# A feed-forward kernel whose mirrored half is finished on VectorE: reading one PSUM bank out in the middle of its sum, in place of splitting the sum over two banks

## The chip, the cores and the metric

The kernel runs on one core of one Trainium2 chip. The metric is device time in microseconds (us) of one execution. The four runs of the kernel before lie within 0.35% (629.28 to 631.47 us). A verdict needs 2%: below that the word is "same", and we then go by the interval of the ratio.

TensorE is written PE in the profile, its weight loads PEld, VectorE DVE, ScalarE ACT, GpSimd POOL and SyncE SP; "POOLq" and "SPq" are their queues as issuers of DMAs. PSUM is the memory that the matmuls of these kernels sum into; a bank here is one tile of it, 128 x 512 numbers (`xb` in the profile).

## The reference, cut to what matters

```python
def _attn_ref(x):                       # x: 8 x 3008 x 256
    X = np.fft.fft(x, axis=1)
    X = np.fft.fft(X, axis=2)
    return X.real.astype(np.float32)

def _moe_ref(x, w_in, w_out):           # 24064 x 256, 256 x 2048, 2048 x 256
    h = np.maximum(x @ w_in, 0.0)
    return (h * h @ w_out).astype(np.float32)
```

The real part of a two-dimensional Fourier transform has mirrored rows. The row at frequency k and the row at S−k share the same two partial sums, one even (a cosine part, called `pt`) and one odd (a sine part, `qt`). The hidden layer is then `even + odd` for the one row and `even − odd` for the mirror. The kernel computes the two partial sums once and makes both rows from them.

## The kernel before: the parts that matter

The work after the transform goes in 25 chunks of columns (numbered from 0; the full ones are 512 pairs wide, the first two 256 and the last 264). Each full chunk has 16 steps, and in each step one unit of 128 hidden features is started, the unit of two steps ago is finished, and eight small matmuls (`po`) of the second layer for the chunk before are mixed in. There are two ways to make a unit.

```python
def x_front(c, u):                       # the normal unit: one bank, three passes of TensorE
    xb = psx.tile(...)                   # one PSUM bank of six
    ... mm(xb, G1, PT) ; mm(xb, G2, QT)  # even + odd
    act(r_s(c, u), xb, AF.Relu)          # ScalarE: first half of h
    return (c, u, xb, None)

def x_back(cur):                         # two steps later (LAG = 2)
    ... mm(xb, G3, QT)                   # G3 = -2*G2: even - odd, in the same bank
    relu_d(c, u, lambda o, i: act(o, xb[:, :, i], AF.Relu))   # ScalarE: mirrored half

def x_split(c, u):                       # the split unit: two banks, two passes
    ... mm(xo, G2, QT) ; mm(xe, G1, PT)
    act(bs[0], xo, AF.Copy)              # ScalarE: odd part to SBUF
    def add():                           # VectorE, one step later
        stt(out=bs[1], in0=ebc[c], scalar=gE2[:, u:u+1], in1=bs[0], op0=mult, op1=subtract)
        sat(r_s(c, u), xe, bs[0])        # saturating add: relu(even + odd)
        relu_d(..., sat(o, xe, bs[1]))   # saturating add: relu(even - odd)
    return (c, u, None, add)
# ... (cuts)
YZ = [(0,0)]*3 + [(2,0)]*3 + [(5,1)]*9 + [(7,1)]*9 + [(0,0)]   # split units, ScalarE squares, per chunk
```

A split unit saves TensorE one pass and costs VectorE three operations. `eb` (`ebc[c]`) is the last row of `qt` copied over all partitions, and its product with `gE` repairs one feature row that carries a different sign. VectorE also squares h (`h<-h`, 128x2048) and makes the transform of the next batches. In the timelines read here VectorE works in the order of the program, whatever has to wait: in run 1 below it stands still for 3.25 us before one saturating add, and behind that add waits a piece of the transform (`v<-u`, started at 330.14 us) whose operand had been complete since 323.64 us.

Of the kernel before, what the change touches and what calls it, by code (L numbers as in the profile page):

```python
# [10 lines left out]
F32 = mybir.dt.float32  # L11
# [13 lines left out]
def kernel(  # L25
# [103 lines left out]
    for s in range(2):  # L129
        gather(0, 1 - s)  # L130
        nc.sync.dma_start(out=x4[0:NP, s, :, :], in_=up(0, s))
    jrow = iota("jrow", [P, P], [[1, P]], 1, 0)
    idx2 = iota("idx2", [P, 1], [[0, 1]], NQ // 2 * (NP - 1), -NQ // 2, I32)
# [56 lines left out]
    def dmats():  # L190
        pv = nc.gpsimd
        t = tgp.tile([P, P], F32, name="td", tag="td")
        m = tgp.tile([P, P], F32, name="md", tag="md")
        pv.tensor_scalar(out=m, in0=jrow, scalar1=pidx[:, 0:1], scalar2=None, op0=ALU.mult)
        pv.tensor_scalar(out=t, in0=m, scalar1=1.0 / D, scalar2=R23, op0=ALU.mult, op1=ALU.add)
        pv.tensor_scalar(out=t, in0=t, scalar1=R23, scalar2=-float(D),
                         op0=ALU.subtract, op1=ALU.mult)
        pv.tensor_tensor(m, m, t, op=ALU.add)
        pv.memset(csD[:, 0, 0, P - 1 : P], 1.0)

        def fin():
            absval(t, m)
            nc.vector.tensor_copy(csD[:, 0, 1, P - 1 : P], alt)
            act(csD[:, 0, 1, 0 : P - 1], m[:, 0 : P - 1], AF.Sin, bias=0.0, scale=wD)
            act(csD[:, 0, 0, 0 : P - 1], t[:, 0 : P - 1], AF.Sin, bias=hpi[:, 0:1], scale=-wD)

        def hi():
            ts(out=csD[:, 1, :, 0:P:2], in0=csD[:, 0, :, 0:P:2], scalar1=-1.0, scalar2=None,
               op0=ALU.mult)
            nc.vector.tensor_copy(csD[:, 1, :, 1:P:2], csD[:, 0, :, 1:P:2])  # L210
        return fin, hi
# [88 lines left out]
    def gmat(c):  # L300
        cs = slice(c * 512, (c + 1) * 512)
        pc = psx.tile([P, 512], F32, name="pc", tag="x")
        for t in range(2):
            mm(pc, cosD[:, t, :], win16(c)[:, t, :], t == 0, t == 1)
        ps = psx.tile([P, 512], F32, name="ps", tag="x")
        for t in range(2):
            mm(ps, sinD[:, t, :], win16(c)[:, t, :], t == 0, t == 1)
        act(G1[:, cs], pc, AF.Copy, bias=0.0, scale=1.0 / HS)
        act(G2[:, cs], ps, AF.Copy, bias=0.0, scale=-1.0 / HS)

# [3 lines left out]

    eall = const.tile([P, 2, NQ, B], F16, name="eall")
    bf = {}
# [88 lines left out]
    def stage1_ops(b, blk, inline_e=False, run=3):  # L405
# [31 lines left out]
        return ops  # L437

    def e_ops(bs):
        nb = len(bs)  # L440
# [14 lines left out]
        for blk in range(2):  # L455
            ops += dft_ops(blk, lambda par, blk=blk: [
                (nb, lambda q: eall[k, blk, q, bs[0] : bs[0] + nb], q, cosT)
                for q in range(par, NQ, 2)], nb, (None, fin(blk)))
# [23 lines left out]

    YZ = [(0, 0)] * 3 + [(2, 0)] * 3 + [(5, 1)] * 9 + [(7, 1)] * 9 + [(0, 0)]

    def plan(c, y, z):
        if chunks[c][1] != CH:
            return (), ()
        return ([u for u in range(NFC) if (u * y + 8) % NFC < y],
                [p for p in range(NFC // 2) if (p * z + 4) % (NFC // 2) < z])

    PLAN = [plan(c, *YZ[c]) for c in range(len(chunks))]

# [7 lines left out]
    def e_double():  # L500
        ts(out=gE2, in0=gE, scalar1=2.0, scalar2=None, op0=ALU.mult)

# [9 lines left out]
    def mm2_ops(c):  # L512
# [48 lines left out]
        def one(grp, j, fc):  # L561
            s, t0, m = grp[j]

            def f():
                if j == 0 and fc == 0:
                    st["o"] = pso.tile([P, 2, D], F32, name="po", tag="po")
                o = n + n % P + t0 if s == 1 else t0
                w = 2 * m if s == 2 else m
                mm(st["o"][0:w, j, :], h2v(c, fc // nf)[:, fc % (2 * nf), o : o + w], wout16[:, fc, :],
# [25 lines left out]
    def x_front(c, u):  # L595
# [3 lines left out]
        for j in range(nf):  # L599
            fs = slice((u * nf + j) * P, (u * nf + j + 1) * P)  # L600
            for sn, G in ((0, G1), (1, G2)):
                for (b, i, o, l) in segs:
                    mm(xb[:, j, o : o + l], G[:, fs], PQ[b][sn][:, i : i + l],
                       j == 0 and sn == 0 and o == 0, sn == 1)
        act(r_s(c, u), xb, AF.Relu)  # L605
        return (c, u, xb, None)
# [3 lines left out]
    def e_spread(c):  # L610
        g0, n, nf, segs = chunks[c]
        ebc[c] = esp.tile([P, CH], F16, name="eb", tag="eb", bufs=2)
        for (b, i, o, l) in segs:
            nc.gpsimd.dma_start(out=ebc[c][:, o : o + l],  # L614
                              in_=PQ[b][1][P - 1 : P, i : i + l].unsqueeze(1).to_broadcast([1, P, l]))

    nsplit = [0]

    def x_split(c, u):
        g0, n, nf, segs = chunks[c]  # L620
        fs = slice(u * P, (u + 1) * P)
        xs = [psx.tile([P, 512], F32, name=nm, tag="x")[:, 0:n] for nm in ("xo", "xe")]
        for t, G, sn in ((xs[0], G2, 1), (xs[1], G1, 0)):
            for (b, i, o, l) in segs:
                mm(t[:, o : o + l], G[:, fs], PQ[b][sn][:, i : i + l], o == 0, True)
        nsplit[0] += 1
        bs = tgp.tile([P, 2, CH], F32, name="bs", tag=("tt", "tm")[nsplit[0] % 2])
        bs = [bs[:, j, 0:n] for j in range(2)]
        act(bs[0], xs[0], AF.Copy, bias=0.0, scale=1.0)  # L629

        def add():
            stt(out=bs[1], in0=ebc[c][:, 0:n], scalar=gE2[:, u : u + 1], in1=bs[0], op0=ALU.mult,  # L632
                op1=ALU.subtract)

            def sat(o, t):
                nc.vector._custom_dve(TENSOR_ADD_SAT, out=o, in0=xs[1], in1=t, s0=BIG, s1=0.0)  # L636

            sat(r_s(c, u)[:, 0, :], bs[0])
            relu_d(c, u, lambda o, i: sat(o[:, 0, :], bs[1]))
        return (c, u, None, add)  # L640

    def x_back(cur):
        c, u, xb = cur[:3]
        if xb is None:
            return
        g0, n, nf, segs = chunks[c]
        for j in range(nf):
            fs = slice((u * nf + j) * P, (u * nf + j + 1) * P)
            for (b, i, o, l) in segs:
                mm(xb[:, j, o : o + l], G3[:, fs], PQ[b][1][:, i : i + l], False, True)  # L650
        relu_d(c, u, lambda o, i: act(o, xb[:, :, i], AF.Relu))  # L651

    def x_square(cur):
# [3 lines left out]
        h2 = h2v(c, u)  # L657
        if u // 2 in PLAN[c][1]:
            nf = chunks[c][2]
# [74 lines left out]
    ST1 = {0: (0.66, 0.98)}  # L734
    EGRP = {1: [2, 3, 4], 4: [5, 6, 7]}
    for b in range(B - 1):
        s0 = first_step[b]
        L = first_step[b + 1] - s0
        at = lambda z: s0 + int(z * (L - 1))
        for bb, lo, hi in FOLD.get(b, []):  # L740
            spread(sum(fold_ops(bb), []), at(lo), at(hi))
        side.setdefault(at(0.0) + 1, []).append(lambda bb=b + 1: alloc_pq(bb))
# [10 lines left out]
    for si, (c, u) in enumerate(steps):  # L753
        if u == 0 and PLAN[c][0]:
            side.setdefault(si - 3, []).append(lambda c=c: e_spread(c))

# [15 lines left out]
    for si, (c, u) in enumerate(steps):  # L772
# [4 lines left out]
        take = [mmq.pop(0) for _ in range(-(-len(mmq) // max(1, due - si)))]  # L777
        flight.append((x_split if u in PLAN[c][0] else x_front)(c, u))
        h = len(take) // 2
# [10 lines left out]
        if len(made) > SQ:  # L790
            retire()
        if len(flight) > 1 and flight[-2][3]:
            flight[-2][3]()
        for f in side.get(si, []):
            f()
    if flight[-1][3]:
        flight[-1][3]()
    while flight:
# [42 lines left out]
```

## Time and profile before

| | before |
|---|---|
| time, median of the runs beside the changed kernel | 630.06 us (629.28 to 631.47) |
| TensorE busy | 606.4 us of a span of 628.5 |
| VectorE busy | 536.8 us |
| ScalarE busy | 479.3 us |
| TensorE, 396 to 588 us | 192.00 of 192 us |

First the busy times of the whole page, and the shares of the chain of work that ended last (the chain is followed back from the last instruction, at each step to what released it):

```profile
PE 606.4 (96%) x4682; PEld 446.9 (71%) x4682; DVE 536.8 (85%) x827; ACT 479.3 (76%) x872; POOL 68.8 (11%) x97
...
PE 92%; DVE 6%; ACT 1%; issue 0%; DVEq 0%; POOL 0%; POOLq 0%; ACTq 0%
```

Next the table of windows for one long late stretch. The columns are the window, its length, then the busy time of PE, PEld, DVE, ACT and POOL with counts, the granted clock, the DMA share and GB/s:

```profile
396.00:588.00 192.00, 192.00 (x1505) 146.25 (x1504) 180.16 (x243) 149.67 (x258) 4.83 (x9) 1.00 0.30 50
```

TensorE has no gap. VectorE is busy for 94% of the stretch.

The groups of VectorE instructions that matter (busy us, mean ns of one | idle before them, and what ended most of it):

```profile
L663 DVE TENSOR_TENSOR h<-h 128x2048 f16<-128x2048 f16 (+1 forms) x174 | 207.8, 1195 | 41.1 <-ACT h L651 36.5
L636 DVE CUSTOM_DVE_ANT_0 h<-xe,bs 128x512 f16<-128x512 f32 x228 | 145.9, 680 | 0.0
L632 DVE SCALAR_TENSOR_TENSOR bs<-eb,gE,bs 128x512 f32<-128x512 f16 x114 | 85.0, 745 | 9.1 <-ACT bs L629 8.4
```

The means are the lengths of single records. What an instruction costs its engine is the distance to the next start when the next one waits for nothing. In this trace that is 1135 ns for the square, 600 for the saturating add and 663 for the add L632: each about 82 ns less than its record.

Last, the timeline around one group of narrow matmuls. The weights `eall` are 127 rows by 3 columns here:

```profile
142.95 0.60 PE L73 MATMUL po<-wout,h 128*128 128x256 f16 x4
143.48 0.64 PE L73 MATMUL pf<-cosT,eall 127*3 127x377 f16 x3
144.06 0.39 PE L73 MATMUL xb<-pt,G 128*128 128x512 f16 x1
```

Four `po` matmuls stand 109 ns apart, so the next should start at 143.39; it starts at 143.48. The same happens on the way back to full-width weights. I count 18 such changes, 1.75 us in all.

### The profile page before, as it was taken

To read this page: it belongs to the slowest core of one execution; us is meant where nothing else is said; L and a number is where in the kernel's file an instruction comes from. 1 tells how busy PE (TensorE), PEld (TensorE's weight loads), DVE (VectorE), ACT (ScalarE), POOL (GpSimd) and SP (SyncE) were. 2 spreads that over 40 slices of the span, in tenths; PEclk is the share of its full clock that TensorE was granted. 3 is DMA by queue.
4 is the path that set the end of the run, shared out by engine and by line. 5 is a ranking of instruction groups with operands and counts; after the bars stand their busy time and mean duration, and the time that the engine had idled before them with its cause. 6 is when DMAs were issued, how large, how long until landed. Compare 5 with 4: busy or idle time off the path is not lost.

```text
span 628.5 us, 11983 instructions
## 1 busy us (share of the span) xinstructions
PE 606.4 (96%) x4682; PEld 446.9 (71%) x4682; DVE 536.8 (85%) x827; ACT 479.3 (76%) x872; POOL 68.8 (11%) x97
## 2 busy tenths in 40 slices
PE   3969999999999999999999999999999999999997
PEld 1547677776777777777777768777787778877786
DVE  8788799995988989889899879998999899999920
ACT  6768887777788788777887877877877778878871
POOL 8204043120120005000000000000000000000000
PEclk9979999999999999999999999999999999999999
DMA  8944477682591416714313314314233134131112
GB/s 282 300 83 138 120 181 205 156 225 57 91 208 36 59 44 170 138 34 59 43 51 44 57 34 63 43 47 48 54 56 43 51 43 59 52 46 48 52 52 68
DMA packets 37342, 57.21 MB, mean 91 GB/s; under 512 B 7262, under 2 KB 31490, under 8 KB 37286
## 3 DMA queue, kind: packets, MB, share of 16 engines
q0 software_dynamic: 7536, 30.21, 27.9%
q1 hardware_dynamic: 29702, 26.23, 13.4%
q8 instruction: 36, 0.59, 0.4%
q14 instruction: 20, 0.16, 0.1%
q10 hardware_dynamic: 48, 0.02, 0.0%
HBM read 29.02 MB, written 24.64 MB: 85 GB/s over the span
## 4 chain that ended last, share of the span: by engine, by line
PE 92%; DVE 6%; ACT 1%; issue 0%; DVEq 0%; POOL 0%; POOLq 0%; ACTq 0%
PE po L73 52%; PE xb L73 25%; PE pf L73 6%; PE xo L73 4%; PE xe L73 4%; DVE h L663 2%; PE warm L73 1%; DVE u L330 1%; DVE v L342 0%; DVE w L348 0%; DVE wout L723 0%; DVE tm L248 0%; ACT h L605 0%; DVE tm L236 0%; DVE tt L183 0%
## 5 line engine op out<-in xcount | busy, mean ns | idle before, releaser
L73 PE MATMUL po<-wout,h 128*128 128x256 f16 x3024 | 433.6, 273 | 0.0
L73 PEld LDWEIGHTS <-h 128*128 128x128 f16 x3024 | 287.2, 98 | 113.9 <-issue 0.4
L663 DVE TENSOR_TENSOR h<-h 128x2048 f16<-128x2048 f16 (+1 forms) x174 | 207.8, 1195 | 41.1 <-ACT h L651 36.5
L605 ACT ACTIVATE h<-xb 128x512 f16<-128x512 f32 (+1 forms) x270 | 159.2, 590 | 67.8 <-PE xb L73 67.1
L73 PE MATMUL xb<-qt,G 128*128 128x512 f16 (+11 forms) x720 | 203.6, 322 | 4.9 <-ACT h L605 4.1
L651 ACT ACTIVATE h<-xb 128x512 f16<-128x512 f32 (+2 forms) x286 | 160.4, 567 | 20.3 <-PE xb L73 13.9
L73 PEld LDWEIGHTS <-G 128*128 128x128 f16 x1384 | 130.3, 98 | 36.7 <-issue 9.6
L636 DVE CUSTOM_DVE_ANT_0 h<-xe,bs 128x512 f16<-128x512 f32 x228 | 145.9, 680 | 0.0
L73 PE MATMUL xb<-pt,G 128*128 128x512 f16 (+9 forms) x360 | 103.8, 324 | 0.3 <-DVE qt L424 0.2
L632 DVE SCALAR_TENSOR_TENSOR bs<-eb,gE,bs 128x512 f32<-128x512 f16 x114 | 85.0, 745 | 9.1 <-ACT bs L629 8.4
L629 ACT ACTIVATE bs<-xo 128x512 f32<-128x512 f32 x114 | 68.5, 601 | 21.0 <-PE xo L73 16.3
L557 ACT ACTIVATE os<-po 128x512 f32<-128x512 f32 x94 | 56.4, 600 | 19.1 <-PE po L73 16.7
L614 POOL DMA_DIRECT2D eb<-qt x28 | 15.4, 551 | 349.6 <-DVE bs L632 297.1
L73 PE MATMUL xo<-qt,G 128*128 128x512 f16 (+14 forms) x152 | 43.4, 327 | 0.0
L73 PE MATMUL xe<-pt,G 128*128 128x512 f16 (+14 forms) x152 | 43.4, 326 | 0.0
L330 DVE TENSOR_TENSOR u<-x 127x765 f16<-127x765 f32 x32 | 29.7, 945 | 0.0
L101 POOL DMA_INDIRECT x<-in_x_dram,idx x18 | 27.6, 1536 | 5.8 <-issue 4.5
L73 PEld LDWEIGHTS <-w 127*128 127x128 f16 (+1 forms) x192 | 21.6, 118 | 7.2 <-issue 1.4
L73 PE MATMUL pf<-cosT,w 127*128 127x377 f16 (+1 forms) x96 | 20.5, 327 | 2.0 <-DVE cosT L279 2.0
L124 POOL DMA_DIRECT2D x<-in_x_dram x14 | 7.9, 562 | 123.3 <-DVE u L334 122.7
L348 DVE TENSOR_TENSOR w<-v 127x381 f16<-127x381 f16 x64 | 20.7, 352 | 0.0
L73 PE MATMUL pf<-sinT,w 127*127 127x377 f16 (+1 forms) x96 | 20.7, 323 | 0.0
(103 smaller groups left out, 216.9 us busy)
## 6 DMA issues: line engine op xcount, KB each, us to landing
out_dram<-os SPq DMA_DIRECT2D x157, 128.0 KB
x<-in_x_dram POOLq DMA_DIRECT2D x14, 756.0 KB, 9.6
wst<-in_moe_w_in_dram POOLq DMA_DIRECT2D x4, 512.0 KB, 6.9
wot<-in_moe_w_out_dram POOLq DMA_DIRECT2D x4, 512.0 KB, 9.1
eb<-qt POOLq DMA_DIRECT2D x14, 128.0 KB, 6.7
x<-in_x_dram SPq DMA_DIRECT2D x2, 756.0 KB
x<-in_x_dram,idx POOLq DMA_INDIRECT x18, 10.7
gE<-G SPq DMA_DIRECT2D x16, 0.2 KB
```

The lines of the kernel that those rows point to most:

```text
L73: nc.tensor.matmul(o, l, r, start=start, stop=stop, skip_group_check=True)
L101: nc.gpsimd.indirect_dma_start(out=x4[0:NP, 2 + s, q : q + rows, :].rearrange("p q d -> p (q d)"), out_offset=None, in_=bass.AP(tensor=x.t ...
L330: return lambda: vt(u[k, s, q0 : q0 + NQ // 2, 1:D], x4[k, s, q0 : q0 + NQ // 2, 1:D], x4[k, 3 - s, ::-1, :][:, q0 : q0 + NQ // 2, D - 1 : ...
L348: return lambda: vt(w[k, i, q : q + 3, 0 : P - 1], vs[s][k, q : q + 3, 1:P], vs[s][k, q : q + 3, D - 1 : P : -1], op=ALU.add if i < 2 else ...
L557: act(os_, po, AF.Copy, bias=0.0, scale=HS * HS)
L605: act(r_s(c, u), xb, AF.Relu)
L614: nc.gpsimd.dma_start(out=ebc[c][:, o : o + l], in_=PQ[b][1][P - 1 : P, i : i + l].unsqueeze(1).to_broadcast([1, P, l]))
L629: act(bs[0], xs[0], AF.Copy, bias=0.0, scale=1.0)
L632: stt(out=bs[1], in0=ebc[c][:, 0:n], scalar=gE2[:, u : u + 1], in1=bs[0], op0=ALU.mult, op1=ALU.subtract)
L636: nc.vector._custom_dve(TENSOR_ADD_SAT, out=o, in0=xs[1], in1=t, s0=BIG, s1=0.0)
L651: relu_d(c, u, lambda o, i: act(o, xb[:, :, i], AF.Relu))
L663: vt(h2, h2, h2, op=ALU.mult)
```

## The change

The intent is to do the split in one bank and with less VectorE work. The even part alone is summed in the bank. VectorE takes it out (`T = -2*even + correction`), TensorE then adds the odd part into the same bank, ScalarE takes the relu of the sum, and one saturating add of the bank and `T` gives the mirror. That leaves VectorE one saturating add instead of two, plus a small multiply for the correction, and more units are taken this way: 152 in place of 114. The copies of `eb` move from GpSimd's queue to SyncE's and stand three steps earlier in the program (two steps later for chunks 6 and 15). Narrow weights are widened to 65 columns. The signs of G1 and G2 are swapped to suit.

The diff, cut to its core:

```diff
-        act(G1[:, cs], pc, AF.Copy, bias=0.0, scale=1.0 / HS)
-        act(G2[:, cs], ps, AF.Copy, bias=0.0, scale=-1.0 / HS)
+        act(G1[:, cs], pc, AF.Copy, bias=0.0, scale=-1.0 / HS)
+        act(G2[:, cs], ps, AF.Copy, bias=0.0, scale=1.0 / HS)
...
+    MW = P // 2 + 1
+    eflat = const.tile([P, 2 * NQ * B + MW], F16, name="eall")
...
-                (nb, lambda q: eall[k, blk, q, bs[0] : bs[0] + nb], q, cosT)
+                (MW, lambda q: ewide((blk * NQ + q) * B + bs[0]), q, cosT)
...
-    YZ = [(0, 0)] * 3 + [(2, 0)] * 3 + [(5, 1)] * 9 + [(7, 1)] * 9 + [(0, 0)]
+    TAKE = [0] * 3 + [2] * 3 + [7] * 9 + [9] * 9 + [8]
...
-                w = 2 * m if s == 2 else m
+                w = MW if s == 2 else m
...
-            nc.gpsimd.dma_start(out=ebc[c][:, o : o + l],
+            nc.sync.dma_start(out=ebc[c][:, o : o + l],
...
-    def x_split(c, u):
...
+    def x_take(c, u, si):
...
+            mm(xb[:, o : o + l], G1[:, fs], PQ[b][0][:, i : i + l], o == 0, True)
+        X = h2v(c, u)[:, u % 2, n : 2 * n]
+        ts(out=X, in0=ebc[c][:, 0:n], scalar1=gE2[:, u : u + 1], scalar2=None, op0=ALU.mult)
...
+            stt(out=T, in0=xb, scalar=-2.0, in1=X, op0=ALU.mult, op1=ALU.add)
+        return (c, u, xb.unsqueeze(1), T)
...
     def x_back(cur):
+        if T is not None:
+                mm(xb[:, 0, o : o + l], G2[:, fs], PQ[b][1][:, i : i + l], False, True)
+            act(r_s(c, u), xb, AF.Relu, scale=-1.0)
+            relu_d(c, u, lambda o, i: nc.vector._custom_dve(
+                TENSOR_ADD_SAT, out=o[:, 0, :], in0=xb[:, 0, i], in1=T[:, i], s0=BIG, s1=0.0))
...
-            side.setdefault(si - 3, []).append(lambda c=c: e_spread(c))
+            side.setdefault(si - (1 if late else 6), []).append(lambda c=c: e_spread(c))
```

Below, "the multiply" is the `ts` line (`h<-eb,gE`), "the add" the `stt` line (`bs<-xb,h`), and "the second pass" the G2 matmul in `x_back` (`xb<-qt,G`).

More of the change, by code (lines that the diff above doesn't have):

```diff
@@ L131 @@
         nc.sync.dma_start(out=x4[0:NP, s, :, :], in_=up(0, s))
-    jrow = iota("jrow", [P, P], [[1, P]], 1, 0)
+    jm = h2p.tile([P, 3, P], F32, name="jm", tag="h2")
+    jrow = jm[:, 0]
+    nc.gpsimd.iota(jrow, pattern=[[1, P]], base=1, channel_multiplier=0,
+                   allow_small_or_imprecise_dtypes=True)
     idx2 = iota("idx2", [P, 1], [[0, 1]], NQ // 2 * (NP - 1), -NQ // 2, I32)
@@ L191, in dmats @@
         pv = nc.gpsimd
-        t = tgp.tile([P, P], F32, name="td", tag="td")
-        m = tgp.tile([P, P], F32, name="md", tag="md")
+        t, m = jm[:, 1], jm[:, 2]
         pv.tensor_scalar(out=m, in0=jrow, scalar1=pidx[:, 0:1], scalar2=None, op0=ALU.mult)
@@ L313, in gneg @@
         ts(out=G3[:, cs], in0=G2[:, cs], scalar1=s3[:, 0:1], scalar2=None, op0=ALU.mult)
-    eall = const.tile([P, 2, NQ, B], F16, name="eall")
+    MW = P // 2 + 1
+    eflat = const.tile([P, 2 * NQ * B + MW], F16, name="eall")
+    nc.gpsimd.memset(eflat, 0.0)
+    eall = eflat[:, 0 : 2 * NQ * B].rearrange("p (s q b) -> p s q b", s=2, q=NQ)
     bf = {}
@@ L437, in stage1_ops, with ewide @@
         return ops
+    def ewide(o):
+        return eflat[k, o : o + MW]
     def e_ops(bs):
@@ L481 @@
         g += n
-    YZ = [(0, 0)] * 3 + [(2, 0)] * 3 + [(5, 1)] * 9 + [(7, 1)] * 9 + [(0, 0)]
+    TAKE = [0] * 3 + [2] * 3 + [7] * 9 + [9] * 9 + [8]
     def plan(c, y, z):
-        if chunks[c][1] != CH:
-            return (), ()
-        return ([u for u in range(NFC) if (u * y + 8) % NFC < y],
+        if chunks[c][2] != 1:
+            return (), (), ()
+        late = chunks[c][3][0][0] in (1, 4) and len(chunks[c][3]) > 1
+        return ([u for u in range(NFC) if (u * y + 8) % NFC < y and not (late and u < 6)], (),
                 [p for p in range(NFC // 2) if (p * z + 4) % (NFC // 2) < z])
-    PLAN = [plan(c, *YZ[c]) for c in range(len(chunks))]
+    PLAN = [plan(c, TAKE[c], (0 if c < 6 else 1)) for c in range(len(chunks))]
     gE = const.tile([P, NFC], F16, name="gE")
@@ L500, in e_double @@
     def e_double():
-        ts(out=gE2, in0=gE, scalar1=2.0, scalar2=None, op0=ALU.mult)
+        ts(out=gE2, in0=gE, scalar1=-2.0, scalar2=None, op0=ALU.mult)
     h2t = {}
@@ L604, in x_front @@
                        j == 0 and sn == 0 and o == 0, sn == 1)
-        act(r_s(c, u), xb, AF.Relu)
+        act(r_s(c, u), xb, AF.Relu, scale=-1.0)
         return (c, u, xb, None)
@@ L613, in e_spread @@
         for (b, i, o, l) in segs:
-            nc.gpsimd.dma_start(out=ebc[c][:, o : o + l],
+            nc.sync.dma_start(out=ebc[c][:, o : o + l],
                               in_=PQ[b][1][P - 1 : P, i : i + l].unsqueeze(1).to_broadcast([1, P, l]))
-    nsplit = [0]
-    def x_split(c, u):
+    taken = [0]
+    tbuf = []
+    def x_take(c, u, si):
         g0, n, nf, segs = chunks[c]
-        fs = slice(u * P, (u + 1) * P)
-        xs = [psx.tile([P, 512], F32, name=nm, tag="x")[:, 0:n] for nm in ("xo", "xe")]
-        for t, G, sn in ((xs[0], G2, 1), (xs[1], G1, 0)):
-            for (b, i, o, l) in segs:
-                mm(t[:, o : o + l], G[:, fs], PQ[b][sn][:, i : i + l], o == 0, True)
-        nsplit[0] += 1
-        bs = tgp.tile([P, 2, CH], F32, name="bs", tag=("tt", "tm")[nsplit[0] % 2])
-        bs = [bs[:, j, 0:n] for j in range(2)]
-        act(bs[0], xs[0], AF.Copy, bias=0.0, scale=1.0)
-        def add():
-            stt(out=bs[1], in0=ebc[c][:, 0:n], scalar=gE2[:, u : u + 1], in1=bs[0], op0=ALU.mult,
-                op1=ALU.subtract)
-            def sat(o, t):
-                nc.vector._custom_dve(TENSOR_ADD_SAT, out=o, in0=xs[1], in1=t, s0=BIG, s1=0.0)
-            sat(r_s(c, u)[:, 0, :], bs[0])
-            relu_d(c, u, lambda o, i: sat(o[:, 0, :], bs[1]))
-        return (c, u, None, add)
@@ L642, in x_back @@
-    def x_back(cur):
-        c, u, xb = cur[:3]
-        if xb is None:
+        if not tbuf:
+            tbuf.extend(tgp.tile([P, 2, CH], F32, name="bs", tag=t) for t in ("tt", "tm"))
+        i = taken[0]
+        taken[0] += 1
+        T = tbuf[i // 2 % 2][:, i % 2, 0:n]
+        fs = slice(u * P, (u + 1) * P)
+        xb = psx.tile([P, 512], F32, name="xb", tag="x")[:, 0:n]
+        for (b, i, o, l) in segs:
+            mm(xb[:, o : o + l], G1[:, fs], PQ[b][0][:, i : i + l], o == 0, True)
@@ new lines, in x_take, with x_back @@
+        X = h2v(c, u)[:, u % 2, n : 2 * n]
+        ts(out=X, in0=ebc[c][:, 0:n], scalar1=gE2[:, u : u + 1], scalar2=None, op0=ALU.mult)
+        if u in PLAN[c][1] and si not in xbusy:
+            act(T, xb, AF.Copy, bias=0.0, scale=-2.0)
+            nc.gpsimd.tensor_tensor(T, T, X, op=ALU.add)
+        else:
+            stt(out=T, in0=xb, scalar=-2.0, in1=X, op0=ALU.mult, op1=ALU.add)
+        return (c, u, xb.unsqueeze(1), T)
+    def x_back(cur):
+        c, u, xb, T = cur
+        g0, n, nf, segs = chunks[c]
+        if T is not None:
+            fs = slice(u * P, (u + 1) * P)
+            for (b, i, o, l) in segs:
+                mm(xb[:, 0, o : o + l], G2[:, fs], PQ[b][1][:, i : i + l], False, True)
+            act(r_s(c, u), xb, AF.Relu, scale=-1.0)
+            relu_d(c, u, lambda o, i: nc.vector._custom_dve(
+                TENSOR_ADD_SAT, out=o[:, 0, :], in0=xb[:, 0, i], in1=T[:, i], s0=BIG, s1=0.0))
@@ L645, in x_back @@
             return
-        g0, n, nf, segs = chunks[c]
         for j in range(nf):
@@ L650, in x_back @@
                 mm(xb[:, j, o : o + l], G3[:, fs], PQ[b][1][:, i : i + l], False, True)
-        relu_d(c, u, lambda o, i: act(o, xb[:, :, i], AF.Relu))
+        relu_d(c, u, lambda o, i: act(o, xb[:, :, i], AF.Relu, scale=-1.0))
     def x_square(cur):
@@ L657, in x_square @@
         h2 = h2v(c, u)
-        if u // 2 in PLAN[c][1]:
+        if u // 2 in PLAN[c][2]:
             nf = chunks[c][2]
@@ L735 @@
     EGRP = {1: [2, 3, 4], 4: [5, 6, 7]}
+    xbusy = set()
     for b in range(B - 1):
@@ L740 @@
         for bb, lo, hi in FOLD.get(b, []):
-            spread(sum(fold_ops(bb), []), at(lo), at(hi))
+            ops = sum(fold_ops(bb), [])
+            spread(ops, at(lo), at(hi))
+            if bb + 1 < B:
+                xs = at(lo) + int((at(hi) - at(lo)) * 6 / len(ops))
+                xbusy.update(range(xs - 2, xs + 4))
         side.setdefault(at(0.0) + 1, []).append(lambda bb=b + 1: alloc_pq(bb))
@@ L754 @@
         if u == 0 and PLAN[c][0]:
-            side.setdefault(si - 3, []).append(lambda c=c: e_spread(c))
+            late = any(chunks[c][3][-1][0] == b + 1 != chunks[c][3][0][0] for b in EGRP)
+            side.setdefault(si - (1 if late else 6), []).append(lambda c=c: e_spread(c))
     LAG = 2
@@ L777 @@
         take = [mmq.pop(0) for _ in range(-(-len(mmq) // max(1, due - si)))]
-        flight.append((x_split if u in PLAN[c][0] else x_front)(c, u))
+        flight.append(x_take(c, u, si) if u in PLAN[c][0] else x_front(c, u))
         h = len(take) // 2
@@ L791 @@
             retire()
-        if len(flight) > 1 and flight[-2][3]:
-            flight[-2][3]()
         for f in side.get(si, []):
             f()
-    if flight[-1][3]:
-        flight[-1][3]()
     while flight:
```

## The prediction

> **What bounds the kernel now.** TensorE. The page gives it 606.4 of 628.5 us busy, and the chain of waits is 92% TensorE. The table of windows shows it busy 24.00 of 24 us in every window from 84 to 588 us, granted clock 1.00. VectorE (536.8 us) and ScalarE (479.3 us) are hidden, VectorE narrowly: 22 to 23.5 of 24 us late on.
>
> **What the change removes from TensorE.** A normal unit costs three passes (G1 pt, G2 qt, G3 qt); a unit taken by VectorE (before: "split") costs two. By the two plans, 114 units were split and 152 will be taken: +2 in most chunks of batches 2 to 4 and of 5 to 7, −2 in chunk 15, +8 in the last chunk (264 wide). So 30 passes of 512 and 8 of 264 columns go (44 matmuls, by the instruction order). Start to start in the trace, a 512-column matmul takes 216 ns, a 264-column one 111 ns: 30×0.216 + 8×0.111 = 7.4 us.
>
> Second, weights of 3 and 16 columns become 65 wide. The timeline shows the first matmul after each change between a narrow and a full weight starting 96 to 99 ns late, 18 times: 1.75 us. [...] At 65 columns I expect none. Sum: about 9.1 us, all on the critical path while TensorE stays the bound.
>
> **What moves on the others** (start to start). Per split unit VectorE did one add of 663 ns and two saturating adds of 600: 1.86 us. Per taken unit: a scalar multiply f16 to f16 (the G3 multiply, same shape, takes 268), an add out of PSUM (estimate 600 to 663), one saturating add: about 1.5 us. In a late chunk 7×1.86 = 13.0 becomes 9×1.5 = 13.5; in a middle chunk 5×1.86 = 9.3 becomes 7×1.5 = 10.5. VectorE should be about 94% busy, 540 to 560 us in all. ScalarE loses one 495 ns pass per extra taken unit, about 20 us in all. The row spreads move from GpSimd to the SyncE queue; nobody waited for them. Startup keeps its order; I expect its TensorE gaps and the half-clock spell at 40 to 47 us again.
>
> **New wait.** The bank leaves through VectorE between the G1 and G2 matmuls, so TensorE's second pass, two steps (3 us) later, waits for an in-order VectorE at 94%. Banks per unit fall from two to one but are held longer. I allow about 1 us for stalls where fold work bunches (84 to 130 and 200 to 370 us).
>
> **Prediction: 621.6 us** (−1.4%); range 618.5 to 626.5. Faster by over 2%: 0.06; within 2%: 0.91; slower by over 2%: 0.03.
>
> **What would show each step.** TensorE matmuls 4682 → 4638, busy about 597 us, still about 24.00 of 24 per window. No 97 ns lateness around the row transform. The f16 multiply at 200 to 270 ns spacing, the add out of PSUM at 600 to 660, the saturating add at 600. ScalarE about 457 us. Waits: none of TensorE's second pass on the add above 1 us in total. First 60 us within 1 us of before.
>
> **What would make it wrong.** (1) VectorE cannot keep up: an add out of PSUM of 0.8 us[...] puts it past 100% in middle and late chunks; TensorE would then wait for it, 2 to 10 us. (2) Row spreads behind the stores on the SyncE queue land late: VectorE's multiply stalls, then TensorE. (3) The startup half-clock spell moves or vanishes, up to 3 us either way. (4) 65 columns still drain: +1.75 us.

7.4 us of passes and 1.75 us of late starts make the 9.1 us, of which about 1 us is allowed back for stalls. That no late start would be left at 65 columns was the expectation; no trace had shown it. The changed kernel's trace shows starts 1 to 5 ns late there, and run 7 none over 30 ns. "Drain" means these measured late starts; no view shows what TensorE does in them. The 0.8 us of risk (1) and the 200 ns at which the multiply's range begins are suppositions, not readings: from start to start the add was then measured at 608 ns and the multiply at 450, or 260 where the next instruction does not need it (run 6). The half-clock spell is a granted clock of 0.50 for 6.8 us, from 40.2 us on in the kernel before.

## The result, and the profile after

The changed kernel takes 634.62 us (634.06 to 636.22, four runs) beside 630.06 us. The ratio is 1.0068, with a 95% interval of 1.0048 to 1.0089: a clear small loss where a gain of 1.4% was forecast. Ratios here are taken over runs of the same series; they are not quite the ratios of the medians quoted.

The page's busy times and the chain, after:

```profile
PE 602.0 (95%) x4638; PEld 445.0 (70%) x4638; DVE 554.9 (87%) x948; ACT 459.2 (72%) x828; POOL 49.4 (8%) x70
...
PE 63%; DVE 31%; DMA 2%; ACT 2%; issue 1%; DVEq 0%; POOL 0%; ACTq 0%; POOLq 0%
```

The 44 matmuls are gone (4682 to 4638), as intended. But VectorE now holds 31% of the chain, where it had 6%. The late stretch:

```profile
396.00:588.00 192.00, 185.99 (x1445) 140.31 (x1444) 179.08 (x279) 135.38 (x237) 0.00 (x0) 1.00 0.28 49
```

TensorE now lacks 6 us here, at a granted clock of 1.00. Compare VectorE: 179.08 us busy after, 180.16 before. The busy share gives no hint that VectorE had become the problem. The groups show more:

```profile
L676 DVE TENSOR_TENSOR h<-h 128x2048 f16<-128x2048 f16 (+1 forms) x173 | 206.8, 1196 | 13.4 <-ACT h L664 12.3
L646 DVE SCALAR_TENSOR_TENSOR bs<-xb,h 128x512 f32<-128x512 f32 (+1 forms) x152 | 103.0, 677 | 19.4 <-PE xb L73 3.9 <-PE po L73 0.5
L657 DVE CUSTOM_DVE_ANT_0 h<-xb,bs 128x512 f16<-128x512 f32 (+2 forms) x160 | 102.3, 644 | 17.5 <-ACT h L656 16.5
L641 DVE TENSOR_SCALAR h<-eb,gE 128x512 f16<-128x512 f16 (+1 forms) x152 | 52.0, 342 | 2.6 <-DMA eb<-qt 2.5
...
L73 PE MATMUL xb<-qt,G 128*128 128x512 f16 (+16 forms) x828 | 233.3, 323 | 13.8 <-DVE bs L646 8.8 <-ACT h L614 4.1 <-DVE qt L428 0.7
```

Read the add, L646: 19.4 us of idle time before it, of which only 4.4 are put down to TensorE. The other 15 us have no releaser in the list. Nearly all of it is the 0.1 us that stands before each of the 152 adds, between the multiply and the add that reads its result. And the last line shows TensorE waiting for that add.

How such a wait comes about is seen in the chain of waits, cut to 440 to 447 us (start, length, what):

```profile
439.57 0.69 DVE bs L646
440.26 0.60 DVE h L657
440.86 0.46 DVE qt L431
441.32 0.45 DVE qt L433
441.77 1.13 DVE h L676
442.90 0.28 DVE h L641
...
443.27 0.69 DVE bs L646
443.96 0.60 DVE h L657
444.56 0.27 DVE h L641
...
444.93 0.70 DVE bs L646
445.63 0.04 issue
445.67 0.38 PE xb L73
```

VectorE works without a pause, and at its end stands a TensorE matmul that could have started before. In the same seven microseconds before the change, the chain is TensorE alone.

**Where the time went.** From the start times of the trace I worked out, for each matmul, how late the next one starts: the distance to the next start, less the columns of this matmul at 2.4 columns a ns (which is the slope between 109 ns for 256 and 216 ns for 512 columns in this trace). The parts then add up to the start of the last matmul. "Late starts" are those over 30 ns after the first 550 matmuls (about 98 us), "startup" is everything late among those 550, "small" is the regular 2 to 5 ns.

| us | before | changed |
|---|---|---|
| first matmul | 10.9 | 11.7 |
| columns at 2.4 a ns, without the last matmul | 583.84 | 576.56 |
| startup | 16.4 | 16.5 |
| small | 11.3 | 11.0 |
| late starts | 1.75 (all at narrow weights) | 14.36 (none at narrow weights) |
| sum, and start of the last matmul | 624.2 | 630.1 |

So both expected gains came: 7.3 us of columns and 1.75 us at the narrow weights. They were more than given back by 14.4 us of new late starts, 13.5 of them in front of a second pass. Each of these 33 passes starts 52 to 54 ns after the end of one particular add. With the first-matmul time (0.8 us later, a matter of startup scatter, see below) this is the whole difference of 5.9 us between the two traces. The medians differ by 4.6 us: the profiled run of the changed kernel, 636.22 us, was the slowest of its four.

In the late chunks these passes belong to units 1, 7, 8 and 10, and once to unit 0 (two of 0.05 us at unit 5 left out). The nine taken units of such a chunk are 0, 1, 3, 5, 7, 8, 10, 12, 14: most of the late passes belong to a unit in one of the two neighbouring pairs. The two at unit 10 (0.82 and 0.87 us) stand behind adds of the row transform in VectorE's queue.

### The profile page after: what moved, and what is told of

The parts are those of the page before. It is cut to its first block, busy times and chain, and to the rows that moved or that the text cites. A ratio compares the mean times of both kernels' runs of the same rounds, so it can differ in the third digit from the quotient of the medians.

```text
span 634.4 us, 12001 instructions
## 1 busy us (share of the span) xinstructions
PE 602.0 (95%) x4638; PEld 445.0 (70%) x4638; DVE 554.9 (87%) x948; ACT 459.2 (72%) x828; POOL 49.4 (8%) x70
## 3 DMA queue, kind: packets, MB, share of 16 engines
q0 software_dynamic: 6304, 27.45, 16.9%
## 4 chain that ended last, share of the span: by engine, by line
PE 63%; DVE 31%; DMA 2%; ACT 2%; issue 1%; DVEq 0%; POOL 0%; ACTq 0%; POOLq 0%
PE po L73 35%; PE xb L73 22%; DVE h L676 10%; DVE bs L646 6%; DVE h L657 5%; PE pf L73 4%; DVE h L641 2%; DMA eb<-qt 2%; DVE u L335 2%; PE warm L73 1%; ACT h L656 0%; DVE v L347 0%; DVE w L353 0%; ACT h L614 0%; DVE wout L736 0%
## 5 line engine op out<-in xcount | busy, mean ns | idle before, releaser
L73 PE MATMUL po<-wout,h 128*128 128x256 f16 x3024 | 452.1, 273 | 0.5 <-DVE h L676 0.5
L73 PE MATMUL xb<-qt,G 128*128 128x512 f16 (+16 forms) x828 | 233.3, 323 | 13.8 <-DVE bs L646 8.8
L614 ACT ACTIVATE h<-xb 128x512 f16<-128x512 f32 (+1 forms) x232 | 138.1, 595 | 51.1 <-PE xb L73 50.9
L664 ACT ACTIVATE h<-xb 128x512 f16<-128x512 f32 (+1 forms) x240 | 138.9, 582 | 32.4 <-PE xb L73 26.9
L73 PEld LDWEIGHTS <-G 128*128 128x128 f16 x1340 | 128.2, 98 | 37.1 <-issue 12.0
L73 PE MATMUL xb<-pt,G 128*128 128x512 f16 (+16 forms) x512 | 147.1, 324 | 0.3 <-DVE qt L429 0.2
L656 ACT ACTIVATE h<-xb 128x512 f16<-128x512 f32 (+1 forms) x152 | 89.5, 589 | 63.9 <-PE xb L73 61.1
L646 DVE SCALAR_TENSOR_TENSOR bs<-xb,h 128x512 f32<-128x512 f32 (+1 forms) x152 | 103.0, 677 | 19.4 <-PE xb L73 3.9
L657 DVE CUSTOM_DVE_ANT_0 h<-xb,bs 128x512 f16<-128x512 f32 (+2 forms) x160 | 102.3, 644 | 17.5 <-ACT h L656 16.5
L641 DVE TENSOR_SCALAR h<-eb,gE 128x512 f16<-128x512 f16 (+1 forms) x152 | 52.0, 342 | 2.6 <-DMA eb<-qt 2.5
L101 POOL DMA_INDIRECT x<-in_x_dram,idx x18 | 23.9, 1326 | 5.6 <-issue 4.8
L674 ACT ACTIVATE h<-h 128x1024 f16<-128x1024 f16 (+1 forms) x19 | 19.8, 1040 | 0.0
L673 ACT ACTIVATE h<-h 128x1024 f16<-128x1024 f16 (+1 forms) x19 | 19.5, 1027 | 0.0
```

The lines of the kernel that those rows point to most:

```text
L73: nc.tensor.matmul(o, l, r, start=start, stop=stop, skip_group_check=True)
L101: nc.gpsimd.indirect_dma_start(out=x4[0:NP, 2 + s, q : q + rows, :].rearrange("p q d -> p (q d)"), out_offset=None, in_=bass.AP(tensor=x.t ...
L614: act(r_s(c, u), xb, AF.Relu, scale=-1.0)
L641: ts(out=X, in0=ebc[c][:, 0:n], scalar1=gE2[:, u : u + 1], scalar2=None, op0=ALU.mult)
L646: stt(out=T, in0=xb, scalar=-2.0, in1=X, op0=ALU.mult, op1=ALU.add)
L656: act(r_s(c, u), xb, AF.Relu, scale=-1.0)
```

## The experiments

**The theories.** A: VectorE has no room left. A taken unit costs it 0.45 + 0.61 + 0.60 = 1.66 us from start to start, not 1.5; the 0.45 is the multiply, whose result the very next instruction reads. B: VectorE's fill is not the matter; the hand-off inside a bank costs at each unit. C, on the side: the copies of `eb`, now in SyncE's queue behind the stores, land late. C rests on two waits, of which this is the longer (VectorE, timeline; the bracket is idle time and releaser):

```profile
574.76 1.22 DVE L676 TENSOR_TENSOR h<-h 128x2048 f16<-128x2048 f16 x1
577.81 0.35 DVE L641 TENSOR_SCALAR h<-eb,gE 128x512 f16<-128x512 f16 x1 [1.84 <-DMA eb<-qt]
```

All runs gave correct results. The "late starts" in this section are worked out as above. The stretch from 396 to 588 us is quoted where it decides.

### 1. Fewer taken units (`old_counts`)

```diff
-    TAKE = [0] * 3 + [2] * 3 + [7] * 9 + [9] * 9 + [8]
+    TAKE = [0] * 3 + [2] * 3 + [7] + [5] * 8 + [12] + [7] * 8 + [0]
```

(The numbers 7 and 12 in chunks 6 and 15 give five and seven units there, as before, because those chunks may not use their first six.)

> The changed kernel, but VectorE takes only the 114 units that were split before (5 in most middle chunks, 7 in late ones, none in the last). Theory A (VectorE is full: a taken unit costs it 0.45+0.61+0.60 = 1.66 us start to start, so nine of them, seven squares of 1.13 and the row-transform adds of about 1.2 fill 24.0 of a late chunk's 24.0 us): at seven units about 20.7 us of 24.4, so TensorE's late second passes, 13.3 us in sum in the changed kernel, shrink to under 2 us; time 628 to 630 us (before 630.1, less 1.75 us of narrow-weight drains, plus up to 0.9 us of startup scatter). Theory B (the hand-off itself is the cost: TensorE's second pass needs an add that stands in an in-order queue, at every taken unit, however full the queue): the stalls go only with the number of units, 13.3 x 114/152 = 10 us; time 637 us or more.

Measured: 633.60 us, ratio to before 1.0045 (1.0012 to 1.0077). The time missed A's forecast by 3.6 us. The trace divides the matter:

```profile
396.00:588.00 192.00, 191.82 (x1507) 146.30 (x1505) 166.71 (x248) 147.59 (x256) 0.00 (x0) 1.00 0.29 50
```

In the late stretch TensorE has all but 0.2 us again, as A said. But 4.4 us of late starts in all remained, 3.9 of them in chunks 6 to 12, nearly all at unit 11 or 15. VectorE was far from full there: it was busy for 154.44 of the 192 us from 180 to 372 us. The timeline of one of them shows VectorE waiting, then bunched:

```profile
324.61 0.55 DVE L347 TENSOR_TENSOR v<-u 127x768 f16<-127x768 f16 x1
328.40 0.69 DVE L657 CUSTOM_DVE_ANT_0 h<-xb,bs 128x512 f16<-128x512 f32 x1 [3.25 <-ACT h L656]
329.01 1.22 DVE L676 TENSOR_TENSOR h<-h 128x2048 f16<-128x2048 f16 x1
330.14 0.55 DVE L347 TENSOR_TENSOR v<-u 127x768 f16<-127x768 f16 x1
330.61 0.35 DVE L641 TENSOR_SCALAR h<-eb,gE 128x512 f16<-128x512 f16 x1
331.06 0.69 DVE L646 SCALAR_TENSOR_TENSOR bs<-xb,h 128x512 f32<-128x512 f32 x1
```

The saturating add waited 3.25 us for ScalarE's relu of the same bank. Behind it in the queue stood a square, a piece of the next batch's transform, the multiply and then the add, whose end at 331.75 let the second pass start at 331.81, 0.87 us late. So theory A alone does not explain the middle chunks: there it is a queue that was held up and then had too much in front of the add. A and this belong together as *crowding*: an add has two steps, about 3 us, from its first matmul to its second pass, and it is late whenever what stands before it in VectorE's queue takes longer.

### 2. The multiply two steps earlier (`early_multiply`)

```diff
+        for c2, u2 in steps[si + 2 : si + 3]:
+            if u2 in PLAN[c2][0]:
+                x_mul(c2, u2)          # the multiply alone; x_take then only adds
         if len(flight) > LAG:
             x_back(flight[0])
```

> The changed kernel with all its 152 taken units, but each unit's small multiply is issued two steps earlier on VectorE, so that a saturating add or a square stands between it and the add that reads its result. Theory A: the pair no longer waits inside itself; multiply to next start 450 becomes about 270 ns, 0.18 us saved per taken unit, 27 us of VectorE in all; a late chunk needs 22.4 of 24.0 us; TensorE's late second passes fall from 13.3 to under 4 us; time 622 to 626 us, faster than before by about 1%. Theory B: VectorE's fill does not matter; stalls stay at about 13 us and the time at 634 us.

Measured: 639.67 us, ratio 1.0148 (1.0113 to 1.0182). On its face a flat contradiction of A. The view of waits tells why:

```profile
DVE h L635 <- DMA eb<-qt: 31.3, 12, 4.8
...
PE xb L73 <- DVE bs L655: 10.3, 16, 1.0
```

The earlier multiply needs `eb` earlier, and VectorE stood 31.3 us, 12 times, before copies that had not landed. After 400 us all late second passes over 0.1 us now belong to units 0 and 1 of a chunk, the first to need a new `eb`. But in the middle chunks, where unit 2 is the first, late starts from 168 to 360 us fell from 4.6 us to 1.1 us, and unit 8 was no longer late anywhere. The edit had exposed C before it could show A.

### 3. The old split at the new counts (`before_new_counts`)

```diff
-    YZ = [(0, 0)] * 3 + [(2, 0)] * 3 + [(5, 1)] * 9 + [(7, 1)] * 9 + [(0, 0)]
+    YZ = [(0, 0)] * 3 + [(2, 0)] * 3 + [(7, 1)] * 9 + [(9, 1)] * 9 + [(0, 0)]
```

> The kernel before with its two-bank split, but 7 and 9 split units per chunk in place of 5 and 7 (150 units; last chunk untouched). Theory A: a split unit costs VectorE 0.66+0.60+0.60 = 1.86 us, nine of them and the rest 16.8+7.9+1.2 = 25.9 us a late chunk where TensorE needs about 24.0: VectorE bounds the late chunks, plus about 2 us in each of nine, and the middle ones come near; time 640 to 652 us: the old way of splitting is even worse at the new counts than the new way. Theory B: the old way has no hand-off inside a bank, TensorE loses 36 passes of 0.216 us; time about 622.5 us.

Measured: 655.10 us, ratio 1.0382 (1.0349 to 1.0414), somewhat beyond A's range and far from B's 622.5 us.

```profile
396.00:588.00 192.00, 179.32 (x1370) 132.53 (x1368) 189.88 (x266) 118.62 (x218) 4.83 (x9) 1.00 0.29 46
```

Here VectorE's busy time itself, 189.88 of 192, says that it is full. The new form is thus indeed cheaper for VectorE: at these counts it loses 20 us less than the old one. What the counts ask of VectorE is the point.

### 4. The other order of the two readers of a bank (`sat_first`)

```diff
-            act(r_s(c, u), xb, AF.Relu, scale=-1.0)
             relu_d(c, u, lambda o, i: nc.vector._custom_dve(
                 TENSOR_ADD_SAT, out=o[:, 0, :], in0=xb[:, 0, i], in1=T[:, i], s0=BIG, s1=0.0))
+            act(r_s(c, u), xb, AF.Relu, scale=-1.0)
```

> The changed kernel with the two readers of a finished bank in the other order: VectorE's saturating add stands first and ScalarE's relu waits for it, in place of the saturating add waiting for the relu (16.5 us of VectorE waits in the changed kernel's profile, 23 times). Theory A in full (VectorE full, and those waits part of what fills it): a few us of stalls go, time 628 to 633 us. If those waits fell where VectorE had nothing else to do, or ScalarE's wait now holds up its in-order queue and with it the banks: no gain or worse, 634 to 640 us.

Measured: 664.98 us, ratio 1.0536 (1.0503 to 1.0570), 30 us worse than the changed kernel.

```profile
ACT h L658 <- DVE h L656: 176.6, 136, 4.3
```

The relu and the saturating add only read the bank, and write different halves of h. Still, in the built program the one that comes second waits for the first, and in the changed kernel's trace all 144 full-width saturating adds start at least 31 ns after the end of their relu. No view shows what makes the wait necessary, and no run was made without it. What the run shows is its price: whichever engine comes second inherits the backlog of the first, and ScalarE behind VectorE is the far worse order, with 176.6 us of waits and 45 us of late starts (VectorE behind ScalarE: 16.5 and 14.4).

### 5. The copies back in GpSimd's queue (`rows_on_gpsimd`)

```diff
-            nc.sync.dma_start(out=ebc[c][:, o : o + l],
+            nc.gpsimd.dma_start(out=ebc[c][:, o : o + l],
```

> The changed kernel, but the copies that spread the last row of qt over all partitions (the operand eb of the multiply) are issued by GpSimd's queue again, as before, at their new earlier place; all else as changed. Theory C (copies issued behind the stores in SyncE's queue land late): the two waits of VectorE's multiply for them (2.5 us) and the two longest late second passes (0.77 and 1.49 us, at units 0 and 1 of the last full chunk) go; the other late passes, at units that follow a taken unit by one step, stay; time 631 to 633.5 us. If C has no part: 634.6 us as changed.

Measured: 630.56 us beside 629.57 us for the kernel before in that series, ratio 1.0014 (0.9987 to 1.0040). Late starts fell from 14.4 to 11.4 us, so C is worth 3.0 us. VectorE waits for no copy any more. Of the two longest late passes the one of 0.77 us went and the one of 1.49 us fell to 0.32; those at unit 1 of chunks 18, 19 and 21 shrank too. The time fell a little more than that; startup was 2.3 us shorter in this profile, which is scatter (see the end). The late passes at units 1, 7, 8, 10 and 11 stayed, as expected.

The traces also show why the copies were late. In the changed kernel SyncE issues the copy for a late full chunk only 6.2 to 8.4 us before the copy's first use, although the program has it earlier than before; in this run GpSimd issues it 23.6 to 30.1 us ahead, and in the kernel before 24.1 to 29.3. Where the landing can be told the copies take about as long on either queue: 5.7 to 8.0 us in these chunks of this run, and 6.1 to 8.3 us in run 2, where the multiply starts as its copy lands. So it was the issue that came late. On SyncE's queue the copies stand behind the stores of results, and these wait for ScalarE to write `os` (the queue's own waits in the changed kernel: us in total, times, longest):

```profile
SPq L555 <- ACT os L566: 391.9, 81, 12.4
```

### 6. Both (`early_and_gpsimd`)

```diff
+        for c2, u2 in steps[si + 2 : si + 3]:
+            if u2 in PLAN[c2][0]:
+                x_mul(c2, u2)
...
-            nc.sync.dma_start(out=ebc[c][:, o : o + l],
+            nc.gpsimd.dma_start(out=ebc[c][:, o : o + l],
```

> Both edits: multiply issued two steps early, and its operand's copies issued by GpSimd's queue. The run with the early multiply alone had lost its stalls in the middle chunks (4.9 to 1.1 us) and at the adjacent units 7 and 8, but waited 31 us for 12 late copies. Theory A+C (crowding of VectorE's queue, made by the 450 ns dependent pair, and late copies; nothing else): VectorE waits for no copy, TensorE's late second passes sum to under 3 us, time 622 to 626 us, about 1% faster than before. If the hand-off itself costs (theory B) 634 us or more.

Measured: 622.24 us, ratio 0.9877 (0.9847 to 0.9908): faster than before by 1.2%, and within 0.7 us of the original forecast for the change. The edit between run 5 and run 6 is only the place of the multiply, and it took late starts from 11.4 to 1.07 us, 8.3 us of the time. VectorE around a pair of neighbours, then the stretch:

```profile
437.60 0.69 DVE L655 SCALAR_TENSOR_TENSOR bs<-xb,h 128x512 f32<-128x512 f32 x1
438.20 0.68 DVE L666 CUSTOM_DVE_ANT_0 h<-xb,bs 128x512 f16<-128x512 f32 x1
438.80 0.68 DVE L655 SCALAR_TENSOR_TENSOR bs<-xb,h 128x512 f32<-128x512 f32 x1
439.39 0.34 DVE L635 TENSOR_SCALAR h<-eb,gE 128x512 f16<-128x512 f16 x1
439.65 1.22 DVE L685 TENSOR_TENSOR h<-h 128x2048 f16<-128x2048 f16 x1
```

```profile
396.00:588.00 192.00, 192.00 (x1509) 146.87 (x1507) 181.00 (x292) 142.76 (x250) 4.81 (x9) 1.00 0.31 51
```

TensorE has its 192 us back, while VectorE is busy for 181.00 us, more than in the changed kernel (179.08). All 152 hand-offs inside a bank are still there, so theory B falls. The multiply at 439.39 is followed after 260 ns by an instruction that does not need it. In the changed kernel the distance from the multiply to the add is 450 ns (median of 144). That is 0.19 us a unit, 29 us in all, and the adds of neighbours come that much earlier. The edit also moves the multiply's own 260 ns out from before its add; no run tells the two parts apart.

### 7. The widening alone (`before_wide`)

The kernel before with the lines of the change about `MW` and `eflat`, and nothing else:

```diff
-                (nb, lambda q: eall[k, blk, q, bs[0] : bs[0] + nb], q, cosT)
+                (MW, lambda q: ewide((blk * NQ + q) * B + bs[0]), q, cosT)
...
-                w = 2 * m if s == 2 else m
+                w = MW if s == 2 else m
```

> The kernel before with one part of the change alone: weights of 3 and 16 columns widened to 65. The 18 drains of 96 to 99 ns go: 1.75 us, ratio 0.997, time 628.5 us against 630.3 us. If the widening costs something elsewhere, or the drains were hidden: 630.3 us.

Measured: 628.13 us, ratio 0.9969 (0.9945 to 0.9992). Its trace has no late start over 30 ns after startup. The same group of matmuls in the changed kernel, for comparison with the lines shown of before:

```profile
143.88 0.60 PE L73 MATMUL po<-wout,h 128*128 128x256 f16 x4
144.31 0.65 PE L73 MATMUL pf<-cosT,eall 127*65 127x377 f16 x3
144.80 0.38 PE L73 MATMUL xb<-pt,G 128*128 128x512 f16 x1
```

144.31 is 0.43 us after 143.88, four times 109 ns: nothing is lost.

### 8. Eight evenly spaced units (`eight_even`), and seven in pairs (`seven_paired`)

Both stand on run 5 (copies by GpSimd, multiply not early). The first has eight taken units a late chunk, at 1, 3, 5, ..., 15. The second has seven in the late full chunks, at 0, 1, 4, 5, 8, 9, 12. The expectation counts chunks from one, where this text counts from zero.

```diff
-    TAKE = [0] * 3 + [2] * 3 + [7] * 9 + [9] * 9 + [8]
+    TAKE = [0] * 3 + [2] * 3 + [7] * 9 + [8] * 9 + [8]             # eight_even
+    TAKE = [0] * 3 + [2] * 3 + [7] + [5] * 8 + [12] + [7] * 8 + [0]  # seven_paired, and:
+        if y == 7 and c > 15:
+            return ([0, 1, 4, 5, 8, 9, 12], (), [4])
```

> The changed kernel with rows spread by GpSimd's queue, multiply not early, and eight taken units a late chunk in place of nine, so that they stand at every second step (1,3,5,...,15) and no two are neighbours. VectorE needs 8 x 1.66 + 7.9 + 1.2 = 22.4 of 24.2 us, about what the early multiply needs at nine. Crowding: the 6.7 us or so of late second passes in late chunks fall under 1 us, the middle chunks keep their 4.6 us; TensorE does 8 passes more (1.7 us); time 625 to 628 us. If neighbours are not what matters: late stalls above 3 us and 629 us or more.

> The changed kernel with rows spread by GpSimd's queue, multiply not early, 114 taken units as before, but in the late full chunks (17 to 24) the seven stand in pairs of consecutive steps (0,1,4,5,8,9,12) in place of every second or third step. The run old_counts, with seven spread out, had no late second pass in those chunks. Fullness alone (VectorE at 20.7 of 24.4 us a chunk): again under 0.5 us of late second passes there; time 629 to 631 us. Crowding (an add behind the neighbour's saturating add and a square in an in-order queue misses its two steps, however much time there is on average): late second passes at units 1, 5 and 9 of 0.1 to 0.5 us each, over 3 us in the eight chunks; time 632 to 637 us.

Measured: 627.20 us, ratio 0.9950 (0.9931 to 0.9968), for eight; 634.36 us, ratio 1.0061 (1.0044 to 1.0078), for the pairs. The stretch of each, eight first:

```profile
396.00:588.00 192.00, 192.00 (x1509) 146.44 (x1507) 178.09 (x268) 147.66 (x253) 5.35 (x10) 1.00 0.31 51
```

```profile
396.00:588.00 192.00, 190.90 (x1501) 145.49 (x1499) 164.10 (x251) 143.24 (x254) 4.81 (x9) 1.00 0.30 50
```

With eight the late chunks have no late start at all, and the middle ones keep their 4.6 us. VectorE's busy time of 178.09 us is all but that of the changed kernel, 179.08; what differs is one unit a chunk and the neighbours. No run has eight units with neighbours, so the share of each is not told apart.

The pairs came out in the crowding theory's range of time, but not for its reason. The trace has 5.5 us of late starts, of which 4.4 are the ones that `old_counts` has too, in chunks 6 to 12 and 15, where both take the same units. The pairs added one late pass of 1.09 us, at unit 1 of chunk 16. The other 23 of the 24 pairs were in time. The late one comes after units 8, 9, 10, 12, 13 and 14 of chunk 15 and unit 0: eight taken units in ten steps, and VectorE works without a gap over 0.11 us from 397 us until that add ends at 411.67. So neighbours alone do no harm: at seven a chunk the queue empties in between. Neighbours in a queue that has not emptied can. This expectation failed in its mechanism, and the theory is narrowed by it.

### 9. More units (`early_gpsimd_more`, `early_gpsimd_most`)

Run 6 with 8 and 10 units and two squares a chunk on ScalarE; then with 9 and 11 units and three squares.

```diff
-    TAKE = [0] * 3 + [2] * 3 + [7] * 9 + [9] * 9 + [8]
+    TAKE = [0] * 3 + [2] * 3 + [8] * 9 + [10] * 9 + [8]    # most: [9] * 9 + [11] * 9
-    PLAN = [plan(c, TAKE[c], (0 if c < 6 else 1)) for c in range(len(chunks))]
+    PLAN = [plan(c, TAKE[c], (0 if c < 6 else 2)) for c in range(len(chunks))]    # most: 3
```

> The two edits, and one more taken unit in each full chunk from the seventh on (8 in the middle, 10 late), with two squares of each such chunk on ScalarE in place of one. TensorE loses about 17 more passes of 0.216 us (3.7 us); VectorE per late chunk 10 x 1.47 + 6 x 1.13 + 1.2 = 22.7 us of 23.8. Theory A+C: 619 to 624 us, the fastest. If more adjacent taken units crowd the queue or ScalarE's extra square (1.9 us a chunk) delays its relus: 624 to 632 us.

> The best version so far (early multiply, rows by GpSimd, 8 and 10 taken units, two squares on ScalarE; 619.1 us) pushed one step further: 9 and 11 taken units, three squares a chunk on ScalarE. TensorE loses about 17 passes more (3.7 us). VectorE 11 x 1.47 + 5 x 1.13 + 1.2 = 23.0 of 23.6 us: if that is still room enough 616 to 618 us; if the queue is full 618 to 625 us.

Measured: 619.14 us, ratio 0.9831 (0.9807 to 0.9855), and 622.96 us, ratio 0.9882 (0.9865 to 0.9898). Columns fell to 572.9 and 569.3 us; late starts rose to 2.6 and 9.7 us. In the second they stand mostly before a `po` matmul (8.5 us in sum), which waits for a square on ScalarE (the view below lists the longer of these waits):

```profile
PE po L73 <- ACT h L683: 5.8, 11, 0.7
```

The first is the best kernel: 1.7% faster than before. The second went past the point, though not for the reason expected: it is ScalarE's squares that came late, not a full queue of VectorE.

## Why the prediction was wrong, point by point

- *TensorE bounds the kernel before; 7.4 us of passes go.* Right: 44 matmuls, 7.3 us of columns. That TensorE would still be busy for all of every window was wrong (185.99 of 192 us late on).
- *The narrow weights' 18 late starts go, 1.75 us.* Right: 1.75 to 0 in the trace, 0.3% alone in run 7. At 65 columns the starts at the same 18 changes were 1 to 5 ns late in the changed kernel, where they had been 95 to 101. What TensorE does in the 97 ns no view shows.
- *ScalarE about 457 us; VectorE 540 to 560 us in all.* Right: 459.2 and 554.9 us. A right busy time was not enough.
- *"I allow about 1 us for stalls."* This is the step that failed. Late starts measured 14.4 us. Moving the copies' queue took away 3.0 of them (run 5) and moving the multiply a further 10.3 (run 6); with both the time was 622.24 us, where 621.6 was forecast for the change as it stood. That is another kernel, so the agreement does not make the forecast right; it fits the other terms of its sum.
- *Why it failed, first term: "a scalar multiply f16 to f16 (the G3 multiply, same shape, takes 268)".* Mis-sized. The 268 ns were read where the next instruction does not depend on the multiply; here the next one reads its result and starts 450 ns after it. A unit costs 1.66 us, not 1.5, and nine cost 14.9 us, not 13.5. The add (608 ns) and the saturating add (598) were sized rightly. Risk (1) of the prediction also named a slow multiply, but looked for it in the length of the instruction itself, which is as forecast where nothing waits for it (260 ns to the next start in run 6).
- *Second term: the two steps.* The prediction saw that TensorE's second pass would wait for an in-order VectorE "at 94%", and then set a busy share against a deadline. Before, VectorE was 94% busy in the late stretch and TensorE had no gap in its 192 us. That banks in reserve took up VectorE's delays there is inference. (It fits run 3, where VectorE is full: 28 of 35.5 us of late starts stand before matmuls that open a bank.) After, each taken unit's add has two steps. At the same busy share TensorE lost 6 us in the late stretch. Nine units with two neighbouring pairs, the 450 ns between multiply and add, and held-up saturating adds made some adds late.
- *Risk (2), "row spreads behind the stores on the SyncE queue land late".* It came true, with two waits of the multiply and 3.0 us of late starts, and a further 31 us of waits lay just behind it (run 2). The copies were late because SyncE issued them 6 to 8 us before their use, where GpSimd issues them 24 to 30 us before (run 5).
- *Startup within 1 us.* The first matmul was 0.8 us later, startup lateness the same, and the half-clock spell came again: a granted clock of 0.50 for 6.8 us in both traces, from 40.2 us before and from 41.2 us after.

What stays open: in the middle chunks at the old counts (run 1) the late passes are told from one timeline, where the saturating add waits behind ScalarE's relu. No run took that wait alone away: run 4 only turned the order of the two readers round. That the early multiply removed three quarters of the middle chunks' late starts at the new counts is shown (run 2); the relu's share in them is argued.

## What to carry to other kernels

When a change makes the bounding engine wait in the middle of a sum for another engine, ask for the deadline of each hand-off and what stands before it in the other engine's queue; that engine's busy share, the same 94% before and after, says nothing. Cost an instruction by the distance to the next start in the order in which it will stand: one whose result the next one reads cost 450 ns here against 260, and moving it two steps up gave 8 us back. A fix that fails may have uncovered the next limit: look at what the trace says it waits for (here the copies) before dropping the theory.

## What the traces show of the hardware

- On VectorE an instruction that waits for nothing started about 82 ns before the record of the one in front ended (the adds of the changed kernel: 608 ns from start to start, records of 690), and the add that waits for the multiply right before it started 104 ns after its end. From start to start the multiply took 450 ns there, against 260 in run 6 (medians of 144 and 115 cases).
- At each of the 18 changes between a weight of 3 or 16 columns and a full one the next matmul started 95 to 101 ns late, and at 65 columns 1 to 5 ns (other matmuls: 2 to 5). No width between 16 and 65 was run.
- Where two engines read one finished bank, the second waited for the first: in the changed kernel the saturating add started at least 31 ns after its relu ended. The second took over the first one's backlog (16.5 us of waits for VectorE behind ScalarE, 176.6 us the other way round).
- What differs between the two queues is the issue: behind SyncE's waiting stores the copies for the late full chunks were issued 6.2 to 8.4 us before their first use, on GpSimd's queue 23.6 to 30.1 us. Moving all 29 took away 3.0 us of late starts, and 31.3 us of VectorE's waits in run 2 went to none in run 6.
- The startup scatters: in profiles of kernels whose first 98 us hold nearly the same program, the first matmul starts between 10.9 and 11.7 us and the startup lateness sums to between 14.8 and 16.9 us. Differences of one or two us between single profiles should not be explained.
